# A hand-planned DeltaNet and MLP kernel on one core: the order of SP's and POOL's transfers, waits of transfers on TensorE, and the PSUM bank of two joins

## The chip, the cores and the metric

The kernel runs on one core of one Trainium2 chip. The metric is the device time in microseconds (us). The engines are named as the profile names them: PE (TensorE's products) with PEld (its weight loads), DVE (VectorE), ACT (ScalarE), POOL (GpSimd), and SP (SyncE, which here only issues transfers).

## The reference

```
k_n = k / (norm(k) + 1e-6)                          # per token
for t in range(S):
    y[t]  = q[t] @ state                            # y before the update
    old   = k_n[t] @ state
    state = state + beta[t] * outer(k_n[t], v[t] - old)
x  = y, heads side by side                          # (B, S, 384)
xn = (x - mean) / sqrt(var + 1e-6) * g_ln
out = x + relu(xn @ w_ch1) @ w_ch2                  # 384 -> 1536 -> 384
```

B = 4, H = 8, S = 768, D = 48, everything in float32. The first part is a recurrence over 768 tokens for each of the 32 pairs of batch and head; the second is a layer norm and a two-layer perceptron for each of the 3072 tokens.

## The kernel before, in words

**Chunks.** The recurrence is cut into 12 chunks of 64 tokens. Within a chunk it becomes matrix algebra: a Gram product of the keys (G, line 963, called by `gram`, line 978), products of queries and keys (also line 963), an inverse X of a unit triangular 64x64 matrix for each head, and then from the state: what the state gives for keys and queries (line 1160), the update u from X (lines 1196 and 1215), the output y (line 1222) and the state's increment (line 1232). The twelve states follow one another: a chunk's u needs the state that the chunk before has left. After y come the layer norm (lines 1266 to 1278), the transposes of its result (line 1310, on PE for chunks 0 to 2, by transfers for the later ones) and the perceptron `mlp(c)`: its first layer (line 1483 for c < 3, line 1416 with fewer products and more sums for the later), a relu on ACT (line 1492), and the second layer (line 1505 for c = 0, line 1584 for the later).

**The inverse, in three ways.** For chunk 0 it is made on PE by doubling: pairs of products E1, Z1 to E5, Z5 (lines 915 and 930), each in two halves, with masks on DVE (line 920), transposes on DVE (line 879) and copies on ACT (line 873) between them. For all other chunks it is made by rows on DVE, for 128 blocks at once (`rows_inverse`, line 1014): the Gram matrix is stored to memory (`gd<-gsb`), its diagonal blocks are gathered back by eight transfers so that each partition holds one block (`gb<-gd`), ACT takes the square root of the diagonal, the keys' norms (line 1026), DVE scales (lines 1027 to 1037) and works through the rows (line 1045 and 1050, in turn), and the result is stored (`xd<-xb`, line 1054) and gathered to its place (`xt<-xd`, line 1058). Chunk 1 has blocks of 16 rows, which `blocks_join` (line 1063, products at 1077 and 1082) makes into blocks of 32; chunks 2 and 3, 4 and 5, and so on are done in twos, in blocks of 32. `join` (line 1098) puts two blocks of 32 together: product e (line 1110), a copy on ACT, product z (line 1115), a copy on ACT. Its PSUM bank is `f2`, one of the perceptron's own, for chunks below `LATER` = 6, and half of `by`, where y is made, for the others; for these it is also emitted with the chunk's own step and not with `rows_inverse`.

**Weights.** They are held as words: ACT fetches pieces of 768 KB (`words<-in_moe_w_ch_dram`), and ACT (lines 730 and 738), DVE (735) and POOL (748) turn each into `w_sb`.

**What sets the order.** The program is not written in the order in which it runs. Class `Line` (line 75) is a planner: every group of instructions is added as a step with its engine, a cost, the keys that it reads and writes, a lag (so long it is held after its inputs are ready) and `t0`, the earliest time that the plan may start it. Due dates for the perceptrons (the list DUE; its last entry is URGENT, the margin from which an overdue small step goes ahead of a perceptron's products) are counted backwards to priorities. `run` then simulates the five engines, the rings of transfers, and the turns of 8 transfer semaphores, and picks steps one after another; in gaps on PE it puts filler products that compute nothing (`zeros`, line 1662). `emit` writes the steps sorted by planned start, and `in_this_order` (line 25) fixes that order on each engine. So a changed cost, lag, `t0` or due date acts on the chip only through the order of the instructions. `t0` of a transfer moves it in the plan and so in its queue; on the chip nothing holds it once its queue reaches it and its data and its semaphore are free.

SP issues nearly all transfers in one queue: raw keys (`load_raw`, four transfers for a chunk), q and v, blocks of q (`load_blocks`), `beta_b`, Gram stores, gathers, outputs. POOL issues the blocks of k for chunks 4 and up, between its own arithmetic, and ACT the words. All stand at line 555, the helper `dma`; a transfer is known in the trace by its names.

In before the raw keys of chunk 2 (to `kr`) and chunk 3 (to `tb`) have `t0` 27 and 29; of the eight gathers of chunk 1 six stand ahead of them in SP's queue and two behind.

Of the kernel before, what the change touches and what calls it, by code (L numbers as in the profile page):

```python
# [18 lines left out]
BK = 32  # L19
# [33 lines left out]
def dve(n):  # L53
    return 0.16 + 1.04e-3 * n
# [20 lines left out]
class Line:  # L75
# [313 lines left out]

        self.steps = every + self.fills  # L390

    def emit(self):
        for s in sorted(self.steps, key=lambda s: (s.start, s.n)):
            s.fn()


@with_exitstack
def kernel(
# [20 lines left out]
    nc = tc.nc  # L419
# [9 lines left out]
    TURNED = 4  # L429
    LNPE = 2  # L430
    GP = 2 * NP
    FROM, LATER = 3, 6
    TOK = 256
    WN = 768

# [76 lines left out]
    xld = dram.tile([128, KC, 4, 2 * BK], FP32, name="xld")  # L512
    xds = [dram.tile([128, BK, BK], FP32, name=f"xd{i}") for i in range(2)]

    line = Line()
    add = line.add
    TWO, BY = ([(n, b, g) for b in range(2) for g in range(2)] for n in ("two", "by"))
# [33 lines left out]

    def dma(eng, out_, in_, n, ns, r=(), w=(), **kw):

        cost = 0.65 if eng != "SP" else 0.45 if n <= 512 else 0.62
        add(eng, cost, lambda: QUEUE[eng].dma_start(out=out_, in_=in_), r, w, bulk=n * ns / 16e3, **kw)  # L555


# [382 lines left out]
    def turned(c, i, dst, dkey, **kw):  # L940
        add(
            "DVE", 1.24,
            lambda: nc.vector.transpose(  # L943
                dst.rearrange("p i (u t) -> p i u t", t=BK), tb[i].rearrange("p (h u d) -> p h u d", u=2, d=BK)
            ),
            tb_keys(i, "blk"), [dkey + (g,) for g in range(2)], **kw,
        )

    def key_half(c, hp, e):
# [64 lines left out]
    def rows_inverse(L, chunks, beta_l, xd, **kw):  # L1014
        gv, xv = (t.rearrange("p s t -> p (s t)")[:, 0 : L * L].rearrange("p (s t) -> p s t", t=L) for t in (gb, xb))
        gbk = [("gb", n) for n in range(8)]
        nb, ns = GH * L, 13.7 if L == BK else 11
        add("Pool", 0.1 + 0.85e-3 * L * L, lambda: nc.gpsimd.memset(xv, 0.0), [], ["xb"], after=MASK_SCRATCH, **kw)
        for n, (p0, c, rows, cols) in enumerate(spots(L, chunks)):
            dma(  # L1020
                "SP", gv[p0 : p0 + GH], gds[c % NG][rows, :, cols].rearrange("s h t -> h s t"),
                nb, ns, [("gd", c % NG)], [("gb", n)], **kw,
            )
        diag = lambda t: t.rearrange("p s t -> p (s t)")[:, 0 :: L + 1]
        nrm, db = nrm_b[:, 0:L], db_b[:, 0:L]
        add("ACT", 0.25, lambda: nc.scalar.sqrt(nrm, diag(gv)), gbk, ["nrm_b"], **kw)
        add("DVE", 0.15, lambda: nc.vector.tensor_scalar_add(nrm, nrm, 1e-6), [], ["nrm_b"], port=2, **kw)
        add("DVE", 0.35, lambda: nc.vector.reciprocal(nrm, nrm), [], ["nrm_b"], port=2, **kw)
        add("DVE", 0.2, lambda: nc.vector.tensor_tensor(out=db, in0=nrm, in1=nrm, op=ALU.mult), ["nrm_b"], ["db_b"], port=1, **kw)
        add(  # L1030
            "DVE", 0.2, lambda: nc.vector.tensor_tensor(out=db, in0=db, in1=beta_l[0], op=ALU.mult),
            beta_l[1], ["db_b"], port=1, **kw,
        )
        add("Pool", 0.25, lambda: nc.gpsimd.tensor_copy(out=diag(xv), in_=db), ["db_b"], ["xb"], **kw)  # L1034
        add(
            "DVE", dve(L * L),
            lambda: nc.vector.tensor_tensor(out=gv, in0=gv, in1=db[:, None, :].to_broadcast([128, L, L]), op=ALU.mult),
            ["db_b"], gbk, port=1, **kw,
        )
        for j in range(L - 1):  # L1040
            n, w = j + 1, L - 1 - j

            def row(j=j, n=n, w=w):
                t = tmp[:, 0 : n * w].rearrange("p (s t) -> p s t", t=w)
                nc.vector.tensor_tensor(  # L1045
                    out=t, in0=xv[:, 0:n, j : j + 1].to_broadcast([128, n, w]),
                    in1=gv[:, j : j + 1, j + 1 : L].to_broadcast([128, n, w]), op=ALU.mult,
                )
                rest = xv[:, 0:n, j + 1 : L]
                nc.vector.tensor_tensor(out=rest, in0=rest, in1=t, op=ALU.subtract)  # L1050

            add("DVE", 2 * dve(n * w), row, gbk, ["xb"], port=1, **kw)
        xdv = xds[xd].rearrange("p s t -> p (s t)")[:, 0 : L * L].rearrange("p (s t) -> p s t", t=L)
        dma("SP", xdv, xv, 128, 25 + L * L * 0.15, ["xb"], [("xd", xd)], **kw)
        for n, (p0, c, rows, cols) in enumerate(spots(L, chunks)):
            if L < BK:
                cols = slice(cols.start % BK, cols.start % BK + L)
            dma(
                "SP", xts[c % NX][rows, :, cols], xdv[p0 : p0 + GH].rearrange("h s t -> s h t"),
                nb, ns, [("xd", xd), ("xz", c % NX)], [("xq", c % NX, n % 8 if L < BK else n % 4)], **kw,  # L1060
            )

    def blocks_join(c, **kw):

        gs, xtc = gsbs[c % NG], xts[c % NX].rearrange("p h (b t) -> p h b t", b=2)
        gk = [("g", c % NG, g) for g in range(2)] + [("go", c % NG, e) for e in range(2)]
        xq = [("xq", c % NX, n) for n in range(8)]
        pe_, pz_ = (p.rearrange("p (h t) -> p h t", t=BK) for p in (f_[2], by[:, 0]))
        XN, ES = ([(n, 0), (n, 1)] for n in ("xn", "es"))
        XT = [("xt", c % NX, g) for g in range(2)]  # L1070
        add("DVE", dve(512), lambda: nc.vector.transpose(xnj, xtc[:, :, 0]), xq + XT, XN, **kw)

        def prod_e():
            for h in range(GH):
                for a in range(4):
                    b = BK * (a % 2)
                    nc.tensor.matmul(pe_[quad(a), h], gs[quad(a), h, b : b + BK], xnj[quad(a), h])

        def prod_z():
            for h in range(GH):  # L1080
                for a in range(4):
                    nc.tensor.matmul(pz_[quad(a), h], es[quad(a), h], xtc[quad(a), h, 0])

# [14 lines left out]
    def join(c, **kw):  # L1098
# [4 lines left out]
        add("DVE", dve(512), lambda: nc.vector.transpose(xnj, xt[:, :, 0:BK]), xq + [("xz", c % NX)] + [("xt", c % NX, g) for g in range(2)], [("xn", 0), ("xn", 1)], **kw)  # L1103
        p = bank.rearrange("p (h t) -> p h t", t=BK)
        c0 = 0 if c == 1 else BK

# [26 lines left out]
    def norms(c, **kw):  # L1133
        i = c % 2
        flat = gpads[c % NG].rearrange("p h t -> (p h t)")
        w = GH * C
        for e in range(2):
            own = flat[e * C * w : e * C * w + C * (w + 1)].rearrange("(s x) -> s x", x=w + 1)[:, 0:w:C]
            dma(
                "SP", ksum[i][half(e)], own, GH * C, 11, [("gd", c % NG)], [("ks", i, e)],  # L1140
                t0={1: 60.0, 2: 90.0, 3: 120.0}.get(c, 0.7), **kw,
            )
        kk = [("kn", i, n) for n in range(2)]
        add("ACT", 0.22, lambda: nc.scalar.sqrt(knrm[i], ksum[i]), [("ks", i, e) for e in range(2)], kk, **kw)
# [196 lines left out]
        return fbanks[turns[0] % 2] if not turns[1] else fbanks[turns[1] % 3]  # L1341


    DUE = [44.40, 70.70, 90.32, 129.22, 162.45, 201.63, 231.70, 268.25, 308.70, 351.43, 392.84, 417.04, 2.36, 1.27, 1.35, 26.71]
    line.URGENT = DUE[15]

    def due(c, t):
# [341 lines left out]
    def prep_g(m):  # L1689
        pr = 20 * m - 15  # L1690
        for c in (2 * m, 2 * m + 1):
            kt = (kts[c % NKT], ("kt", c % NKT))
            if c == 2:
                load_raw(c, pr=pr, t0=27.0)
                first_kt(kraws[2], raw_keys(2), *kt, PAIRS[3], pr=pr, t0=40.0)
            elif c == 3:
                keys = [("tb", 2, e, hp) for hp in range(2) for e in range(2)]
                load_raw(c, dst=tb[2], keys=keys, pr=pr, t0=29.0)
                first_kt(tb[2], keys + [("tbpad", 2)], *kt, PAIRS[3], pr=pr, t0=40.0)
            else:  # L1700
                load_blocks(2 * (c % 2), k, c, "Pool", pr=pr, t0={2: 80.0, 3: 120.0}.get(m, 40.0 * m - 20))
# [14 lines left out]
    for n, (p0, c, rows, cols) in enumerate(spots(BK, (0, 1))):  # L1716
# [1 line left out]
        dma(  # L1718
            "SP", beta_b[p0 : p0 + GH],
            beta[2 * e : 2 * e + 2].rearrange("g h (m s) -> (g h) m s", m=NSL)[:, :, t0 : t0 + BK],  # L1720
            96, 13.7, w=[("beta_b", n)], pr=5, t0=46.0,
        )

    def prep_x(m):
# [16 lines left out]
            join(c, pr=pr, lag=0.5)  # L1741
        recur(c, pr, lag=0.8)

    load_padded(1, q, 1, ("SP", "SP"), pr=8.2, t0=42.0)
    load_v(1, pr=8.1, t0=42.0)
    norms(1, pr=4)
    blocks_join(1, pr=3)
    join(1, pr=3)
# [22 lines left out]
    if PLAN is not None:  # L1771
        PLAN.append(line)
    with in_this_order(tc):
        line.emit()


# [28 lines left out]
```

## Time and profile before

| | |
|---|---|
| median of 5 runs | 560.1 us (558.41 to 561.62) |
| the profiled execution | 559.68 us |
| its span, first to last instruction | 558.0 us |
| mean granted clock of PE | 0.983 |
| PE busy | 527.5 us |
| last product ends | 553.56 us from the span's start |
| `gb<-gd`, 40 issues, 64 KB each in the median | 3.4 us from issue to landing |
| `words<-in_moe_w_ch_dram`, 10 issues, 768 KB | 5.9 us |

The profile is read by the span's own clock: a product "at 65.44" starts 65.44 us after the first instruction. In the chain of work that ended last, each line is a start, a duration and an engine with a line of the code; an engine's name with a q (SPq, ACTq) is the issue of a transfer by that engine, and DMA is the transfer itself. In a row of the timeline the bracket says how long the engine had stood idle and which instruction ended it. "issue" there means that nothing the profile records was waited for. PEclk is the clock that PE was granted, in tenths of full speed.

### The profile page before, as it was taken

The page shows a single profiled execution, that of the slowest core. Times are in us where ns is not written, and L with a number is a line of the kernel's source. Part 1 is how long each engine was busy: PE and PEld are TensorE (multiplying, and loading weights), DVE is VectorE, ACT ScalarE, POOL GpSimd, SP SyncE. Part 2 cuts the span into 40 slices and gives each one's busy share as a digit, 9 for nine tenths or more (in the row PEclk, how much of TensorE's full clock was granted, in tenths as well). Part 3 has the DMA queues.
Part 4 walks back from the last instruction along what each step waited for, and adds up shares of the span by engine and source line. Part 5 has one row for each costly group of instructions (what it writes and reads, how often), then busy time and mean ns, then how long its engine had stood idle before and what let it go on. Part 6 is the DMA issues. An engine that isn't in the chain of part 4 may idle for free.

```text
span 558.0 us, 23060 instructions
## 1 busy us (share of the span) xinstructions
PE 527.5 (95%) x10060; PEld 478.3 (86%) x10060; DVE 366.2 (66%) x884; ACT 191.3 (34%) x452; POOL 253.5 (45%) x399
## 2 busy tenths in 40 slices
PE   8777978999998999899999999999999999999996
PEld 5556756678987799899999999999999999999996
DVE  4686548972689946989858868668778436253331
ACT  4586634232242324232323423413313224323030
POOL 5251438306885656276260362453352612426242
PEclk9798989899999999999999999999999999999999
DMA  9866777188455767553742544734414410111101
GB/s 172 269 144 138 186 197 102 28 188 143 56 80 87 130 177 95 117 100 83 173 68 55 98 78 95 173 45 81 94 23 96 107 30 32 32 56 32 28 1 29
DMA packets 195973, 54.67 MB, mean 98 GB/s; under 512 B 186136, under 2 KB 189344, under 8 KB 195872
## 3 DMA queue, kind: packets, MB, share of 16 engines
q1 hardware_dynamic: 190112, 40.39, 37.6%
q10 hardware_dynamic: 3552, 9.63, 5.4%
q0 software_dynamic: 2208, 3.17, 3.8%
q8 instruction: 79, 1.29, 1.0%
q14 instruction: 22, 0.18, 0.1%
HBM read 36.38 MB, written 16.78 MB: 95 GB/s over the span
## 4 chain that ended last, share of the span: by engine, by line
PE 85%; DVE 5%; DMA 4%; issue 2%; ACT 2%; SPq 1%; POOL 0%; ACTq 0%; DVEq 0%; POOLq 0%
PE f L1584 28%; PE f L1416 25%; PE f L1483 6%; PE two L963 4%; PE f L1505 3%; PE by L1222 2%; PE two L1232 2%; PE by L1160 2%; PE two L1160 2%; PE two L1215 2%; DMA gd<-gsb 1%; DVE tmp L1045 1%; PE by L1110 1%; PE by L1115 1%; DVE xb L1050 1%
## 5 line engine op out<-in xcount | busy, mean ns | idle before, releaser
L1584 PE MATMUL f<-w_sb,h_all 128*128 128x192 f32 x396 | 95.1, 332 | 0.0
L1584 PE MATMUL f<-words,h_all 128*128 128x192 f32 x396 | 93.1, 328 | 0.0
L1570 POOL TENSOR_TENSOR h_all<-h_all 128x256 f32<-128x256 f32 x99 | 73.1, 744 | 40.7 <-PE f L1584 35.6
L1416 PE MATMUL f<-xnt,w_sb 128*128 128x128 f32 x648 | 88.0, 277 | 0.0
L1609 POOL TENSOR_TENSOR words<-h_all 128x128 f32<-128x128 f32 x66 | 30.8, 478 | 117.0 <-ACT h_all L1435 98.0
L1416 PEld LDWEIGHTS f<-xnt,w_sb 128*128 128x128 f32 x648 | 80.1, 192 | 0.7
L1438 DVE TENSOR_TENSOR h_all<-f,h_all 128x256 f32<-128x256 f32 x135 | 56.5, 421 | 33.5 <-PE f L1416 19.6
L1050 DVE TENSOR_TENSOR xb<-xb,tmp 128x60 f32<-128x60 f32 (+19 forms) x170 | 69.9, 411 | 5.8
L1045 DVE TENSOR_TENSOR tmp<-xb,gb 128x60 f32<-128x60 f32 (+19 forms) x170 | 65.9, 387 | 7.1 <-POOL xb L1034 4.5
L1584 PEld LDWEIGHTS f<-words,h_all 128*128 128x128 f32 x396 | 68.3, 190 | 0.4
L1584 PEld LDWEIGHTS f<-w_sb,h_all 128*128 128x128 f32 x396 | 66.4, 190 | 1.8 <-ACT words L1615 0.3
L1483 PE MATMUL f<-xnt,w_sb 128*128 128x256 f32 x216 | 52.5, 393 | 4.8 <-ACT h_all L1492 4.8
L1483 PEld LDWEIGHTS f<-xnt,w_sb 128*128 128x128 f32 x216 | 41.0, 195 | 12.9 <-ACT h_all L1492 4.4
L555 POOL DMA_DIRECT2D tb<-in_k_dram x64 | 41.6, 656 | 7.0 <-DVE kt L943 5.8
L1602 DVE TENSOR_TENSOR o<-f,x 128x192 f32<-128x192 f32 x33 | 11.7, 355 | 47.9 <-PE f L1584 22.8
L1435 ACT ACTIVATE h_all<-f 128x256 f32<-128x256 f32 x54 | 20.6, 381 | 53.4 <-PE f L1416 27.7
L1584 PE MATMUL f<-w_sb,words 128*128 128x192 f32 x132 | 32.5, 330 | 0.6 <-DVE o L1602 0.6
L1602 POOL TENSOR_TENSOR o<-o,words 128x192 f32<-128x192 f32 x22 | 13.3, 624 | 38.6 <-DVE words L1602 38.6
L748 POOL TENSOR_TENSOR w_sb<-words 128x768 uint32<-128x768 uint32 (+1 forms) x11 | 14.9, 1359 | 28.2 <-ACT words L738 18.4
L1492 ACT ACTIVATE h_all<-f 128x256 f32<-128x256 f32 x36 | 13.6, 382 | 38.7 <-PE f L1483 35.1
L1435 ACT ACTIVATE h_all<-h_all 128x256 f32<-128x256 f32 x54 | 22.2, 413 | 10.3 <-DVE h_all L1438 10.2
L825 POOL TENSOR_TENSOR v<-v,knrm 128x768 f32<-128x768 f32 x11 | 16.7, 1519 | 17.6 <-PE f L1416 10.0
(235 smaller groups left out, 940.5 us busy)
## 6 DMA issues: line engine op xcount, KB each, us to landing
words<-in_moe_w_ch_dram ACTq DMA_DIRECT2D x10, 768.0 KB, 5.9
gd<-gsb SPq DMA_DIRECT2D x11, 512.0 KB, 3.5
v<-in_v_dram SPq DMA_DIRECT2D x24, 192.0 KB, 4.5
out_dram<-o SPq DMA_DIRECT2D x48, 96.0 KB, 2.6
kr<-in_k_dram SPq DMA_DIRECT2D x46, 96.0 KB, 3.3
xld<-xlt SPq DMA_DIRECT2D x9, 384.0 KB, 3.6
xnt<-xld SPq DMA_DIRECT2D x36, 96.0 KB, 3.2
gb<-gd SPq DMA_DIRECT2D x40, 64.0 KB, 3.4
```

The source lines that it names most:

```text
L555: add(eng, cost, lambda: QUEUE[eng].dma_start(out=out_, in_=in_), r, w, bulk=n * ns / 16e3, **kw)
L963: nc.tensor.matmul(pair[hp][half(e ^ (hp & n)), (g * NP + j) * C : (g * NP + j + 1) * C], kt[drows(hp), l], rt[drows(hp), i],)
L1045: nc.vector.tensor_tensor(out=t, in0=xv[:, 0:n, j : j + 1].to_broadcast([128, n, w]), in1=gv[:, j : j + 1, j + 1 : L].to_broadcast([128, n ...
L1050: nc.vector.tensor_tensor(out=rest, in0=rest, in1=t, op=ALU.subtract)
L1416: nc.tensor.matmul(wide(p[:, 128 * n : 128 * n + 128]), w[:, f : f + 128], r, start=start and n == 0, stop=stop, skip_group_check=True)
L1435: add("ACT", act(256), lambda: nc.scalar.activation(to[0], p, ACTF.Relu), pk, to[1])
L1438: add("DVE", dve(256), lambda: nc.vector.tensor_tensor(out=to[0], in0=ps(p), in1=y[0], op=op), [*pk, *y[1]], to[1])
L1483: nc.tensor.matmul(p[:, 0:TOK], w1_sb[:, t, f * 128 : (f + 1) * 128], xnt[:, t], start=(t == 0), stop=(t == KC - 1))
L1570: add(eng, cost, lambda: e.tensor_tensor(out=out_, in0=x, in1=y, op=op), r, w, port=2 if eng == "Pool" else 1, pr=-2)
L1584: lambda f=f, t=start and f == 0: nc.tensor.matmul(p[:, 0:D2], lhs(f), rhs[:, f], start=t, stop=(f == F2 - 1), skip_group_check=True),
L1602: lambda: e.tensor_tensor(out=out_, in0=a, in1=b_, op=ALU.add), r, w, pr=pr,
L1609: lambda f=f + i: e.tensor_tensor(out=s3[f], in0=one(0, 0)[0](f), in1=one(1, 0)[0](f), op=ALU.subtract),
```

## The change

1. `emit` gets an additional dependency. If a step is a transfer of SP or POOL (not ACT) with a `t0` above 1.0, and the plan starts it less than 3.0 after its `t0`, it is made to wait on the chip for a PE step: the last among the eight latest PE steps whose planned end is not after the transfer's planned start. 37 transfers get such a wait, among them the raw keys of chunks 2 and 3, q and v of chunk 1, `beta_b`, q, v and the norms' sums of chunks 2 and 3, and the k blocks of chunks 4 to 7 on POOL.
2. `t0` of the raw keys of chunk 2 goes from 27 to 35, of chunk 3 from 29 to 37.5, of q and v of chunk 1 from 42 to 44, of `beta_b` from 46 to 48.
3. A list LAG gives lags to the square root (line 1026) of the first two `rows_inverse`, 2.00 each, and 0.72 to that of the later; the other entries are 0 or what was there before (0.5).
4. The planned cost of an SP issue becomes 0.45 below 384 packets and 0.65 from there (was 0.45 up to 512, else 0.62). Three due dates and URGENT are changed.
5. `LATER` goes from 6 to 4, so that the joins of chunks 4 and 5 use y's bank and come with the chunk's own step.

No product, copy or transfer is added or taken away but for fillers: 29 instructions of them before, 25 after. In the new order SP issues all eight gathers of chunk 1 ahead of the raw keys; then the keys, q and v of chunk 1, part of `beta_b`, the store of chunk 1's inverse (`xd<-xb`) ahead of the gathers of chunks 2 and 3, where it was behind them, and the gathers back (`xt<-xd`) mixed with the rest of those. On PE the transposes of chunk 2's keys and product G2, which stood between the halves of Z4 and of E5, come behind E5, the transposes ahead of Z5 and G2 behind it. On ACT the copies of Z5 come ahead of those of the Gram product and of keys, the square root of chunks 2 and 3 behind most of mlp(0)'s relus, and a fetch of words behind the layer norm's root. On DVE `xln` of chunk 2 comes ahead of a mask product (line 994) and of rows.

```diff
-    def emit(self):
+    def emit(self, tc):
+        block = tc.nc.cur_bb.bb.instructions
+        gate, ends = None, []
         for s in sorted(self.steps, key=lambda s: (s.start, s.n)):
             s.fn()
+            if s.eng == "PE":
+                ends.append((s.end, block[-1]))
+            if s.bulk is not None and s.t0 > 1.0 and s.eng != "ACT" and s.start < s.t0 + 3.0:
+                gate = [i for e, i in ends[-8:] if e <= s.start]
+                if gate:
+                    tc.add_manual_dep(
+                        block[-1], gate[-1].name,
+                        mybir.DependencyInfo(mybir.DependencyClass.Sync, mybir.DependencyReason.DATA), reason="paced",
+                    )
...
-    FROM, LATER = 3, 6
+    FROM, LATER = 3, 4
...
+    LAG = [2.00, 2.00, 0.72, 0.00, 0.50, 0.50, 0.00, 0.00]
...
-        cost = 0.65 if eng != "SP" else 0.45 if n <= 512 else 0.62
+        cost = 0.65 if eng != "SP" else 0.45 if n < 384 else 0.65
...
-        add("ACT", 0.25, lambda: nc.scalar.sqrt(nrm, diag(gv)), gbk, ["nrm_b"], **kw)
+        add("ACT", 0.25, lambda: nc.scalar.sqrt(nrm, diag(gv)), gbk, ["nrm_b"], lag=LAG[min(chunks[0] // 2, 2)], **kw)
...
-    DUE = [44.40, 70.70, 90.32, 129.22, 162.45, 201.63, 231.70, 268.25, 308.70, 351.43, 392.84, 417.04, 2.36, 1.27, 1.35, 26.71]
+    DUE = [44.40, 70.70, 90.32, 129.22, 162.45, 201.63, 230.26, 270.16, 308.70, 352.52, 392.84, 417.04, 2.36, 1.27, 1.35, 23.59]
...
-                load_raw(c, pr=pr, t0=27.0)
+                load_raw(c, pr=pr, t0=35.0)
...
-                load_raw(c, dst=tb[2], keys=keys, pr=pr, t0=29.0)
+                load_raw(c, dst=tb[2], keys=keys, pr=pr, t0=37.5)
...
-            96, 13.7, w=[("beta_b", n)], pr=5, t0=46.0,
+            96, 13.7, w=[("beta_b", n)], pr=5, t0=48.0,
...
-    load_padded(1, q, 1, ("SP", "SP"), pr=8.2, t0=42.0)
-    load_v(1, pr=8.1, t0=42.0)
+    load_padded(1, q, 1, ("SP", "SP"), pr=8.2, t0=44.0)
+    load_v(1, pr=8.1, t0=44.0)
```

The dates and lags in this code are those of the plan; none of them is a measured time.

More of the change, by code (lines that the diff above doesn't have):

```diff
@@ L945, in turned @@
             ),
-            tb_keys(i, "blk"), [dkey + (g,) for g in range(2)], **kw,
+            tb_keys(i, "blk"), [dkey + (g,) for g in range(2)], lag=LAG[6], **kw,
         )
@@ L1070, in blocks_join @@
         XT = [("xt", c % NX, g) for g in range(2)]
-        add("DVE", dve(512), lambda: nc.vector.transpose(xnj, xtc[:, :, 0]), xq + XT, XN, **kw)
+        add("DVE", dve(512), lambda: nc.vector.transpose(xnj, xtc[:, :, 0]), xq + XT, XN, lag=LAG[3], **kw)
         def prod_e():
@@ L1102, in join @@
         xq = [("xq", c % NX, n) for n in range(8)]
-        add("DVE", dve(512), lambda: nc.vector.transpose(xnj, xt[:, :, 0:BK]), xq + [("xz", c % NX)] + [("xt", c % NX, g) for g in range(2)], [("xn", 0), ("xn", 1)], **kw)
+        add("DVE", dve(512), lambda: nc.vector.transpose(xnj, xt[:, :, 0:BK]), xq + [("xz", c % NX)] + [("xt", c % NX, g) for g in range(2)], [("xn", 0), ("xn", 1)], **dict(kw, lag=LAG[4 + (c > 3)]))
         p = bank.rearrange("p (h t) -> p h t", t=BK)
@@ L1143, in norms @@
         kk = [("kn", i, n) for n in range(2)]
-        add("ACT", 0.22, lambda: nc.scalar.sqrt(knrm[i], ksum[i]), [("ks", i, e) for e in range(2)], kk, **kw)
+        add("ACT", 0.22, lambda: nc.scalar.sqrt(knrm[i], ksum[i]), [("ks", i, e) for e in range(2)], kk, lag=LAG[7], **kw)
         add("Pool", 0.2, lambda: nc.gpsimd.tensor_scalar_add(knrm[i], knrm[i], 1e-6), [], kk + [("kn", i)], **kw)
@@ L1773 @@
     with in_this_order(tc):
-        line.emit()
+        line.emit(tc)
 _INS = ['q', 'k', 'v', 'beta', 'moe_g_ln', 'moe_w_ch1', 'moe_w_ch2']
```

## The prediction

> **What bounds the kernel now.** I read the busy shares and the slices first, then the chain that ended last, then the gaps of TensorE and, in the stretch that the change touches, the waits and the chain in order of time. From the page:
>
> ```profile
> PE 527.5 (95%) x10060; PEld 478.3 (86%) x10060; DVE 366.2 (66%) x884; ACT 191.3 (34%) x452; POOL 253.5 (45%) x399
> ...
> PE   8777978999998999899999999999999999999996
> ...
> PEclk9798989899999999999999999999999999999999
> DMA  9866777188455767553742544734414410111101
> ...
> PE 85%; DVE 5%; DMA 4%; issue 2%; ACT 2%; SPq 1%; POOL 0%; ACTq 0%; DVEq 0%; POOLq 0%
> ```
>
> TensorE is the bound: 527.5 us busy of 558.0. A slice is 13.95 us. The holes and the reduced clock lie in the first eight slices, up to 112 us, while the DMA digits are high there; after slice 16 (223 us) the row is all nines. By the gaps between TensorE's instructions some 26 us are idle in all, and only 2.8 us of that after 226 us. No product is added or taken away by the change, so it can gain only what TensorE idles, what its filler products (line 1662) cover, and what half clock costs. That is spent in the first 226 us, and there I stay.
>
> Three stretches matter. The first is chunk 0's inverse, about 38 to 56 us. The timeline rows of TensorE:
>
> ```profile
> 44.65 0.69 PE L915 MATMUL two<-qt,gsb 64*64 64x64 f32 x32
> ...
> 48.69 0.39 PE L963 MATMUL f<-kt 48*64 48x64 f32 x11 [2.53 <-issue]
> ...
> 50.49 0.99 PE L930 MATMUL two<-xt,pt 64*64 64x64 f32 x32 [0.41 <-DVE pt L920]
> ```
>
> The first half of the E5 product (line 915) runs at 44.65, then comes Gram product G2 of the next chunk (line 963), in its middle 2.53 us with nothing waited for (code arriving), and only then E5's second half (48.86) and Z5 (49.40, 50.49 to 51.48). The second is mlp(0), where the chain in order of time reads:
>
> ```profile
> 68.21 1.30 POOL w_sb L748
> 69.51 2.17 DMA xd<-xb
> ...
> 72.05 5.49 DMA xt<-xd
> 77.54 0.02 issue
> 77.56 0.02 ACTq L555
> 77.58 0.04 issue
> 77.61 0.37 ACTq L555
> 77.99 0.05 issue
> 78.03 0.39 ACT h_all L1492
> 78.43 0.04 issue
> 78.47 4.30 PE f L1483 x12
> ```
>
> and the waits of ACT between 60 and 90 us, in sum, times and longest:
>
> ```profile
> ACT nrm_b L1026 <- DMA gb<-gd: 3.4, 1, 3.4
> ACT h_all L1492 <- DMA xt<-xd: 3.4, 1, 3.4
> ```
>
> ACT is queued behind transfers twice. Its square root for chunks 2 and 3 (line 1026, 71.57) stands ahead of a relu of mlp(0) and waits for gathers. Its weight fetch (line 555, 77.61) does not issue until `xt<-xd` has landed, although it shares no data with it: the issues use a limited set of transfer semaphores in turn, and the fetch's turn is held by that gather. TensorE then waits 1.18 us (71.85 to 73.03) and 2.61 us (75.86 to 78.47) for the relu, and the twelve products after the second gap take 4.30 us where the same twelve took 2.86 at 67.92. Nor is `xd<-xb` itself on time: its rows are ready at 60.15 and it is issued at 69.51, because SP spends 59.95 to 69.40 on eight gathers of the next two chunks. The third stretch is between a chunk's output and the next mlp: y1 ends at 109.08 and the first product of mlp(1) starts at 121.93; y2 ends at 161.06 and mlp(2) starts at 173.83.
>
> **The change part by part** (against the profiled 559.68).
>
> *Front: gathers of chunk 1 first, keys of chunks 2 and 3 later; −4.8, bounds −6 to −2.* In SP's queue all eight gathers now stand ahead of the raw keys (before: six at 23.48, the last two at 34.79, behind eight key issues of 0.65). TensorE's new order is Z4's halves without the key transposes between them (1.02 us gone from there), both halves of E5, the transposes, Z5, one filler, G2. From 44.65, less the 1.0 of the transposes, E5, copies and Z5 take what they took without G2's 0.99 + 2.53 ahead of the second half: Z5 ends near 47.2 to 48.2 and not at 51.48, 3.3 to 4.3 earlier. The code still has to arrive; I let half of the 2.53 come back: −3.0. ACT's copies of Z5 (line 873) ended 4.07 us after it (55.55), with a Gram copy and two key copies between them (1.53 waiting for the transposes of line 771); now they stand first: six copies of 0.38, 2.3 us, so −1.8. Ends: all of the code load comes back (−2); none, and all transposes hidden (−6).
>
> *SP's and ACT's queues in mlp(0); −5.2, bounds −5.2 to 0.* The store `xd<-xb` is moved ahead of the gathers of chunks 2 and 3 and the square root behind most of the relus. That removes 1.18 + 2.61 + (4.30 − 2.86 = 1.44). What is late next is the fetch itself, moved behind the LN's root. No gain at all if another transfer holds its turn.
>
> *What is then late: ahead of mlp(1); +4.7, bounds 0 to +4.7.* The 12.85 us between y1 and mlp(1) are filled now. If mlp(0) ran ahead, less of its second layer is left: in the new order seven products of line 1505 stand there (0.71 each: the trace shows two records for each, eight records in 2.85 us), 5.0 us, two Grams at 1.10 and two transposes at 0.49, 8.2 us in all, and seven fillers where there were none. With the way through VectorE, ACT and the transposes as long as it is now, 12.85 − 8.2 = 4.7 come back. Its shortest seen length is y0's: 58.71 to 65.44, 6.73, with which nothing would come back; but VectorE has chunk 1's to 3's rows (lines 1045, 1050) between, so I take the upper end.
>
> *Ahead of mlp(2); −1.4, bounds −3.9 to 0.* The line that carries it:
>
> ```profile
> 171.55 1.05 PE L1310 MATMUL by<-ident,xln 128*128 128x128 f32 x6 [1.40 <-DVE xln L1278]
> ```
>
> VectorE runs a mask product (line 994, 1.22) and two row steps (168.15 to 171.01) ahead of `xln`; in the new order `xln` comes first. The stall goes; up to 3.9 if the fillers shrink too.
>
> *Waits added; +1.1, bounds 0 to +2.6.* 37 transfers of SP and POOL now wait for a TensorE instruction. Behind the waiting issue stands the rest of that queue: at SP q and v of chunk 1, `beta_b`, the Gram store and the gathers; at POOL the last weight conversions (line 748, 1.47 each) behind chunk 4's k blocks, which wait for mlp(0)'s second layer. For the keys of chunk 2 the gates are E4's halves (38.54, 39.05), for those of chunk 3 E4 and Z4; such a transfer lands 3.4 to 4.5 after its issue, so chunk 2's last one by 43 to 45, about when its transposes now come. The trace has no such wait. Nothing, if the keys land in 3.4; the 1.1 between the two landings, if in 4.5; and a conversion more, 2.6, if POOL's queue decides too. I take 1.1, since the transposes come close to the landing and the conversions are wanted only by mlp(1).
>
> *Half clock after a new gap; +1.0, bounds 0 to +1.7.* Gaps of 2.71, 2.53, 2.61 us are each followed by 3.4 us at 0.5 (PEclk over 50 to 54 us 0.59, over 78 to 82 us 0.57), at 1.44 to 1.69 us each. Where the holes ahead of mlp(1) are filled this costs nothing; I take two thirds of one. The Trainium skill (TensorE: Matmul & The Clock Gate, Part 1) names a longer idle window, about 3.4 us, before the clock halves; here gaps of 2.5 to 2.7 were enough. By the page's rule this term would be 0.
>
> *Joins of chunks 4 and 5 in y's bank; 0, bounds −1 to +1.5.* Same products (211.53 to 221.92, both chunks' ahead of y4 at 222.38); now chunk 5's come behind y4. TensorE waited for nothing between them, since products of mlp(2) stand there; in the new order products of the same mlp do. The nearest gaps are 1.51 of code at 223.74, taken as the loss, and two small ones at 255.93 and 336.06 (0.68, 0.64), in sum 1.3, of which a gain of 1 is the most.
>
> Sum: −4.8 − 5.2 + 4.7 − 1.4 + 1.1 + 1.0 + 0 = −4.6, so 555.1 in the profiled execution, and 555.5 as a median, which lies 0.42 above it before (560.1 against 559.68).
>
> The Trainium skill (DMA: Bandwidth & Descriptors, Issuing engines are not separate DMA queues) says that transfers from any engine interleave on the same 16 engines and that more issuing engines save only issue time. Taken alone it speaks against this change, since the bytes stay the same; the store that is ready at 60.15 and issued at 69.51 shows that the order within one queue counts here.
>
> **Rivals.**
>
> *Slower: the held transfers hold ACT.* A gated transfer keeps its turn until its TensorE product is done and its bytes have landed. If ACT reaches its second fetch (now ahead of copies that TensorE needs) while that turn is held, ACT stands still, as at 77.61. Longest landing seen: 9.86 us (`tb<-in_q_dram`, issued at 36.64). Price up to 9.9: −4.6 + 9.9 = +5.3, 565.4. It decides from the point where the transfer lands over 4.6 us after ACT is there. For it: the wait at 77.61, and `beta_b`, whose six issues took 6.98 us from 43.25, 1.16 each against 0.65 of a key, so turns were short there already. Against it: with the keys held back fewer transfers of the front share the engines, and the same bytes may land sooner.
>
> *All given back: about 560.1.* The chain through chunk 1 to 3 may be the true bound, and every microsecond won early turns into fillers; −4.8 − 5.2 come back ahead of mlp(1) and mlp(2). For it: the new fillers. Against it: stalls of 1.18 and 2.61 have nothing to do with that chain.
>
> *More is kept: 550.8.* Nothing comes back ahead of mlp(1), if its way takes nearer 6.73 than 12.85: 555.5 − 4.7.
>
> *The waits do nothing.* Where a transfer is issued later than its product anyway (those held to 105 and 120 in the plan go out from 112 on), the gate is empty; then the order alone acts, and the time is within the first case.
>
> **How the numbers follow.** Likeliest case 0.50 (551 to 558.5; 0.46 faster, 0.04 the same). More kept 0.12, faster. Given back 0.15 (0.02, 0.10, 0.03). ACT held 0.23 (0.03 the same, 0.20 slower). Together faster 0.60, same 0.17, slower 0.23; 0.3%, 1.7 us, is about what a measurement of this kernel can tell from no change. Range 551 to 563: it leaves out the upper part of the held case (0.14) and the lowest of the kept one (0.06). The likeliest case's own range is 551 to 558.5.
>
> **What would show it.** Z5 ends near 48; no wait of line 1026 ahead of a relu and no wait of a fetch on `xt<-xd`; the first product of line 1483 near 60.7; fillers and a gap ahead of mlp(1), which starts about 8 to 13 us after y1; by 300 us the same products come 4 to 5 us earlier than before, and from there on the two traces run in parallel. It is wrong if ACT waits for a transfer anew, if TensorE waits for a key transpose, or if mlp(1) starts where it did.

## The result, and the profile after

| | before | after |
|---|---|---|
| median of all runs | 558.54 us (91 runs, 552.91 to 564.80) | 559.01 us (51 runs, 554.21 to 563.48) |
| ratio to before, 95% interval | | 1.0014 (1.0002 to 1.0027) |
| profiled execution, span | 559.68, 558.0 us | 559.42, 557.6 us |

A drop of 4.6 us was forecast; the change costs 0.8 us (0.14% of 558.5). Runs of one kernel differ by several us, so a ratio rests on many of them, and a difference of two spans is read to about 2 us.

The page of the changed kernel, for the rows shown of before:

```profile
PE 525.7 (94%) x10052; PEld 475.9 (85%) x10052; DVE 367.8 (66%) x884; ACT 191.6 (34%) x452; POOL 257.2 (46%) x399
...
PE   7667998999999999998999999999999999999996
...
PEclk9998998999999999989999999999999999999999
DMA  9846866389365577246671645352524131122101
...
PE 76%; DVE 8%; DMA 7%; issue 3%; POOL 3%; ACT 2%; SPq 0%; ACTq 0%; DVEq 0%; POOLq 0%
```

PE's sixth slice (70 to 84 us) goes from 7 to 9: the waits in mlp(0) are gone. The first three are emptier by one each. In the chain PE has fallen from 85% to 76%; VectorE, transfers and POOL took the place.

Lines of code are 14 higher in the changed kernel (1483 is now 1497), and a few more in some experiments. The timeline of TensorE in the front, changed kernel:

```profile
39.73 0.69 PE L929 MATMUL by<-qt,gsb 64*64 64x64 f32 x32 [0.57 <-ACT xt L887]
43.41 1.06 PE L785 MATMUL f<-ident,kr 128*128 128x128 f32 x8 [2.99 <-DMA kr<-in_k_dram]
44.40 0.89 PE L944 MATMUL f<-xt,pt 64*64 64x64 f32 x32
...
52.97 0.68 PE L1236 MATMUL two<-u,pt 64*64 64x48 f32 x32 [1.47 <-DVE u L1215]
```

E5's second half now runs at 39.73 and not at 48.86, without G2 ahead of it. Then TensorE stands for 2.99 us, because the transposes ahead of Z5 want chunk 2's keys, which a wait had held back. TensorE had been ready for them at 40.42. The waits of ACT between 60 and 90 us, same kernel:

```profile
ACT h_all L1506 <- PE f L1497: 5.6, 6, 2.8
ACT h_all L744 <- DMA beta_b<-in_beta_dram: 1.8, 1, 1.8
ACT nrm_b L1040 <- issue: 1.4, 1, 1.4
```

The two waits of 3.4 are gone. A new one is there: ACT stands 1.8 us until `beta_b` has landed, whose turn its fetch of words needs, and `s_all`, queued behind, comes late; TensorE idles 0.96 us for it at 63.02. That is the rival with the held turns, at a tenth of its price here (0.96 of 9.9; 1.85 in e4 below).

To see where time goes, count for every product the median distance to the next one on its line in before, nothing for fillers, and call what TensorE's time exceeds this by lost. The windows are fixed stretches of the span, so 1 us may belong to a neighbour. The last column is the experiment e4 below.

| us of the span | before | after | e4, keys not held |
|---|---|---|---|
| 0 to 60 | 37.0 | 36.3 | 34.2 |
| 60 to 80 | 9.6 | 2.2 | 3.8 |
| 80 to 110 | 11.1 | 12.1 | 11.3 |
| 110 to 122 | 2.5 | 6.1 | 6.4 |
| 122 to 175 | 14.5 | 15.3 | 14.1 |
| 175 to 270 | 22.6 | 23.9 | 23.0 |
| 270 to the end | 38.7 | 39.7 | 39.4 |
| sum | 136.0 | 135.6 | 132.1 |

By this count 8.1 us are won by 80 us in the changed kernel and given back in several places, the largest 3.6 us ahead of mlp(1). The starts say the same: mlp(0) at 60.27 (65.44 before), y1's end 107.81 (109.08), mlp(1) 120.28 (121.93), mlp(2) 169.43 (173.83). Each column is one execution, and the front of one kernel moves by more than its total: in e16 below, whose order is that of before up to 86 us, TensorE waited 4.42 us for chunk 1's norms (0.51 in before) and mlp(0) started at 69.67, not at 65.44.

### The profile page after: what moved, and what is told of

Read it like the earlier page. It is cut to its first block, busy times and chain, and to the rows that moved or that the text cites. A ratio compares the mean times of both kernels' runs of the same rounds, so it can differ in the third digit from the quotient of the medians.

```text
span 557.6 us, 23081 instructions
## 1 busy us (share of the span) xinstructions
PE 525.7 (94%) x10052; PEld 475.9 (85%) x10052; DVE 367.8 (66%) x884; ACT 191.6 (34%) x452; POOL 257.2 (46%) x399
## 4 chain that ended last, share of the span: by engine, by line
PE 76%; DVE 8%; DMA 7%; issue 3%; POOL 3%; ACT 2%; SPq 0%; ACTq 0%; DVEq 0%; POOLq 0%
PE f L1598 28%; PE f L1430 25%; PE f L1497 4%; PE two L977 3%; DVE xb L1064 2%; DVE tmp L1059 2%; PE by L1236 2%; PE two L1229 2%; PE by L1174 2%; PE two L1174 2%; PE by L1129 2%; PE by L1124 2%; PE two L1246 2%; DMA xt<-xd 2%; DMA words<-in_moe_w_ch_dram 1%
## 5 line engine op out<-in xcount | busy, mean ns | idle before, releaser
L1598 PE MATMUL f<-w_sb,h_all 128*128 128x192 f32 x396 | 97.4, 336 | 0.0
L1430 PEld LDWEIGHTS f<-xnt,w_sb 128*128 128x128 f32 x648 | 79.5, 192 | 3.4 <-issue 1.7
L1064 DVE TENSOR_TENSOR xb<-xb,tmp 128x60 f32<-128x60 f32 (+19 forms) x170 | 73.5, 432 | 5.8
L1497 PE MATMUL f<-xnt,w_sb 128*128 128x256 f32 x216 | 49.8, 383 | 0.0
L1497 PEld LDWEIGHTS f<-xnt,w_sb 128*128 128x128 f32 x216 | 40.2, 190 | 6.0
L1446 ACT COPY h_all<-f 128x256 f32<-128x256 f32 x27 | 10.0, 372 | 44.2 <-PE f L1430 43.7
L839 POOL TENSOR_TENSOR v<-v,knrm 128x768 f32<-128x768 f32 x11 | 16.3, 1483 | 16.4 <-DMA v<-in_v_dram 9.5
```

The source lines that it names most:

```text
L1430: nc.tensor.matmul(wide(p[:, 128 * n : 128 * n + 128]), w[:, f : f + 128], r, start=start and n == 0, stop=stop, skip_group_check=True)
L1497: nc.tensor.matmul(p[:, 0:TOK], w1_sb[:, t, f * 128 : (f + 1) * 128], xnt[:, t], start=(t == 0), stop=(t == KC - 1))
L1598: lambda f=f, t=start and f == 0: nc.tensor.matmul(p[:, 0:D2], lhs(f), rhs[:, f], start=t, stop=(f == F2 - 1), skip_group_check=True),
```

## The experiments

Each was run 6 to 12 times beside before on the same chip; the ratio is to before, with its 95% interval. The changed kernel's own is 1.0014 (1.0002 to 1.0027).

| run | ratio | interval |
|---|---|---|
| e1 no waits | 0.9953 | 0.9925 to 0.9981 |
| e2 waits alone, on before | 1.0041 | 1.0007 to 1.0075 |
| e4 keys of chunk 2 not held | 0.9951 | 0.9916 to 0.9987 |
| e4b the same again | 0.9934 | 0.9903 to 0.9964 |
| e5 gathers back first | 1.0048 | 1.0015 to 1.0081 |
| e6 gathers in first | 1.0012 | 0.9981 to 1.0043 |
| e7 e4 and e5 | 0.9962 | 0.9931 to 0.9993 |
| e3 LATER = 6 in the changed kernel | 1.0230 | 1.0196 to 1.0264 |
| e8 LATER = 4 alone, on before | 1.0122 | 1.0088 to 1.0156 |
| e9 e4, layer norm first, no fillers | 1.0004 | 0.9970 to 1.0037 |
| e10 e4, no fillers | 0.9970 | 0.9935 to 1.0005 |
| e11 e4, layer norm first | 1.0002 | 0.9972 to 1.0032 |
| e12 e4, store of chunk 1 late | 0.9955 | 0.9922 to 0.9988 |
| e13 e4, rows cut, no fillers | 0.9872 | 0.9824 to 0.9921 |
| e14 e4, rows cut | 0.9898 | 0.9862 to 0.9934 |
| e16 rows cut, on before | 1.0025 | 0.9996 to 1.0054 |

**e1, no waits.** The condition for a wait is never true; the order of all engines is that of the changed kernel.

```diff
-            if s.bulk is not None and s.t0 > 1.0 and ...
+            if False and s.bulk is not None and s.t0 > 1.0 and ...
```

> The changed kernel with its order unchanged and the 37 added waits left out. Three theories of where the gain went. A: the inverse of chunk 1 comes back too late (xt<-xd lands 9 us after its first issue), so chunk 1's chain sets mlp(1). B: VectorE, full from 85 us on with rows of chunks 2 and 3, sets it. C: it is lost after 235 us, with the joins of chunks 4 and 5. Here all three expect that the 2.99 us for which TensorE waits for kr go, and that mlp(0) begins up to 3 us earlier than 60.27. A and B expect no more than 1 us of it in the total, since transfers or rows decide later; C expects the 3 us in the total (about 556). If the held transfers made room for others, the gathers land later and it is slower by 1 to 3.

0.9953. The order without the waits is faster than before, the order with them is not; the difference in the total, 0.0061 or 3.4 us, is the size of the 2.99 us that are gone. But its profiled execution does not show it in the front. Where TensorE waited for the keys, two gaps have come in which nothing recorded was waited for:

```profile
45.16 0.21 PE L944 MATMUL f<-xt,pt 64*64 64x64 f32 x1 [2.15 <-issue]
...
49.17 0.26 PE L1210 MATMUL by<-v,xt 64*64 64x48 f32 x2 [1.09 <-issue]
```

mlp(0) starts at 61.99, later than 60.27 and against what all three theories expected.

**e2, the waits alone.** `emit` of the changed kernel put into before.

> The kernel before with only the added waits (its own order, t0 and joins). If the waits by themselves help by keeping transfers apart, words and gathers land sooner and it is 1 to 3 us faster than before. If they only hold SP's queue, it is the same or up to 3 us slower: q, v and beta_b of chunk 1 go out later and push the gathers of chunks 2 and 3, which stood ahead of xd<-xb. Theory A expects slower by the time that xd<-xb goes out after 69.51.

1.0041: the waits help nothing of themselves; 0.4 to 4.2 us slower by the interval. VectorE's transpose for chunk 1's blocks waits 9.0 us for `xt<-xd`, where it waited 5.0.

**e4, one set of four waits.** Only the four transfers of chunk 2's raw keys lose theirs; 33 waits stay.

```diff
-            if s.bulk is not None and s.t0 > 1.0 and ...
+            if s.bulk is not None and s.name != "keys2" and s.t0 > 1.0 and ...
...
-                load_raw(c, pr=pr, t0=35.0)
+                load_raw(c, pr=pr, t0=35.0, name="keys2")
```

> The changed kernel, only the four raw-key transfers of chunk 2 without a wait. They go out behind the last gather at 28 and not from 34.93. TensorE's wait of 2.99 us for kr should go, Z5 end near 43.5 and mlp(0) begin near 57.5. A: rows and xd<-xb earlier by up to 1, total within 1 us of the changed kernel. B: the same. C: 3 us less in the total.

0.9951, and again:

> The kernel with the keys of chunk 2 not held once more, as the reference on the same chip for the next three: about 0.995 of before.

0.9934. Four waits out of 37 carry all that e1 showed. In e4 TensorE goes from E5 to the transposes without a wait:

```profile
41.08 0.69 PE L929 MATMUL by<-qt,gsb 64*64 64x64 f32 x32 [0.57 <-ACT xt L887]
41.71 1.09 PE L785 MATMUL f<-ident,kr 128*128 128x128 f32 x8
```

The same holds over more executions. In the four that hold these keys in the changed front (the changed kernel, e5, e6 and e3 below) TensorE waits 2.99, 3.95, 3.18 and 4.38 us ahead of these transposes and mlp(0) starts at 60.27 to 63.26; in the nine that free them and keep the other waits TensorE waits for no key there and mlp(0) starts at 57.34 to 60.12. SP's queue, first the changed kernel, then e4:

```profile
22.09 5.91 SPq L569 DMA_DIRECT2D gb<-gd  x8
34.93 2.67 SPq L569 DMA_DIRECT2D kr<-in_k_dram  x4
```

```profile
23.20 6.19 SPq L569 DMA_DIRECT2D gb<-gd  x8
29.44 2.63 SPq L569 DMA_DIRECT2D kr<-in_k_dram  x4
```

The queue is empty at 28 in the first and stands until 34.93. And then the keys meet ACT's fetch of 768 KB, issued at 35.94. The median landings, issued between 34 and 44 us in the changed kernel:

```profile
words<-in_moe_w_ch_dram ACTq DMA_DIRECT2D x1, 768.0 KB, 6.1
kr<-in_k_dram SPq DMA_DIRECT2D x4, 96.0 KB, 6.4
```

and between 28 and 44 us in e4:

```profile
words<-in_moe_w_ch_dram ACTq DMA_DIRECT2D x1, 768.0 KB, 4.6
kr<-in_k_dram SPq DMA_DIRECT2D x4, 96.0 KB, 3.8
```

Held to a quiet moment in the plan, the keys went out in a busy one: 6.4 us to landing and not 3.8. The fetch alone does not make that. In e4 the keys of chunk 3 go out beside it (38.20, the fetch at 37.22) and take 4.5; in e1 both sets of keys go out one behind the other, 28.24 to 34.08, ahead of the fetch (36.82), and take 4.2 and 3.8. In the changed kernel both sets and the fetch meet, and all land late: 6.4, 6.8 (chunk 3) and 6.1. The Trainium skill (DMA: Bandwidth & Descriptors, Issuing engines are not separate DMA queues) says that transfers of different issuers interleave on the same engines. That fits; no run here moves the fetch alone.

**e5 and e6, the order of two sets of gathers.** Theory A held that chunk 1's inverse comes back late: its store is issued at 57.44 and not at 69.51, yet VectorE's transpose of the blocks starts at 81.83 (78.73 before). e5 puts all `xt<-xd` ahead of all `gb<-gd` of chunks 2 and 3 in SP's queue, e6 the other way round.

```diff
+        last = max(s.start for s in self.steps if s.name == "back1")
+        for s in self.steps:
+            if s.name == "in2":
+                s.start = max(s.start, last + 1e-3)
         for s in sorted(self.steps, key=lambda s: (s.start, s.n)):
```

> The changed kernel, with all eight gathers back (xt<-xd) in SP's queue ahead of the eight gathers of chunks 2 and 3 (gb<-gd), which stood ahead of and among them. A: xt lands by 70 to 73, the products of line 1091 start near 75 and not at 82.59, y1 ends 5 to 7 us earlier, and the total falls by 3 to 5. B: the square root of chunks 2 and 3 comes after 81.2, rows end later, xln of chunk 1 does not come earlier than 116.9 and the total is the same or up to 3 slower. C: the same.

> The changed kernel with the gathers of chunks 2 and 3 (gb<-gd) all ahead of the gathers back (xt<-xd); the store xd<-xb stays ahead of both. A: xt lands later than now, the products of line 1091 start at 83 to 86, total 1 to 3 slower. B: the square root of chunks 2 and 3 comes up to 8 us earlier than 81.2, VectorE's rows end earlier, xln of chunk 1 near 113, total 1 to 3 faster. C: the same.

In e5 the transpose starts at 73.61, 8 us earlier, and y1 ends at 109.44, 1.6 later than in the changed kernel; the total is not faster (1.0048). Theory A falls as stated, with 3 to 5 us to win. That the way back decides nothing is not shown, because e5 brings a new stall: ACT's square root now waits 3.89 us for the gathers of chunks 2 and 3, a relu stands behind it, and TensorE idles:

```profile
84.91 2.87 PE L1523 MATMUL f<-w_sb,h_all 128*128 128x384 f32 x4 [2.92 <-ACT h_all L1510]
```

In e6 the square root came at 84.08, not earlier as B had it, and the total stayed (1.0012); it told nothing of B. There ACT, with a fetch of words next, stood 5.85 us until a gather had landed, and TensorE 2.50 us for the relu behind it.

**e7, both.**

> The changed kernel with both edits: keys of chunk 2 not held, and gathers back ahead of the gathers in. A: the 3 us of the keys and the 3 to 5 of the gathers add up in part, 4 to 7 us faster than the changed kernel, about 553. B: as with the gathers alone, the same or slower. C: 3 us.

0.9962, no better than e4 alone; the stall of e5 is there again (2.37 us). Against e5, which differs from it only in the four waits, it is 0.0086 or 4.8 us faster by the ratios: freeing these keys pays in a second order too.

**e3 and e8, the joins of chunks 4 and 5.** One constant each, but the plan is made anew with it.

> The changed kernel with LATER = 6 again: joins of chunks 4 and 5 in the bank of the perceptron and with their rows; the order up to chunk 2 is the same. A and B: within 1 us of the changed kernel, since what is lost by 135 us stays lost. C: the 0.88 us of code and the half clock after it (242 to 246) go, about 1.9 us, with some of the gap of 1.72 at 259, so 2 to 3 us faster than the changed kernel.

> The kernel before with LATER = 4 alone. C: slower by 2 to 4, from gaps and half clock behind y4 as in the changed kernel. A and B: within 1 us of before.

Both slower, by 2.3% and 1.2%. Theory C, that the old place would win 2 to 3 us, falls as stated. But in e8 the order has changed from the start (a gap of 5.86 us at 75.81, long before chunk 4), and in e3 from chunk 2 on, with gaps of 2.07 us for POOL's `h_all` at 205.02 and 2.69 us for VectorE's `o` at 262.69. They measure a new plan, not the joins; what the joins alone cost stays open.

**e9 to e11, between y1 and mlp(1).** Theory D, formed here: the order is fixed, so the layer norm's place behind rows and the seven fillers are paid on the chip. All three start from e4.

```diff
+        y = max(s.start for s in self.steps if s.name == "y1")
+        last = max(s.start for s in self.steps if s.name == "xln1")
+        for s in self.steps:
+            if s.name == "row2" and y < s.start < last:
+                s.start = last + 1e-3
         for s in sorted(self.steps, key=lambda s: (s.start, s.n)):
+            if s.name == "fill" and 100.0 < s.start < 114.0:
+                continue
```

> The changed kernel with the keys of chunk 2 not held (as in the kernel with free keys, 0.995 of before), and between y1 and mlp(1) the layer norm of chunk 1 ahead of the rows of chunks 2 and 3 on VectorE, and the seven fillers left out there. Theory D, formed after the first runs: the instruction order is fixed, so what the plan puts between y1 and mlp(1) is paid on the chip: VectorE's rows ahead of xln, and seven fillers. D expects xln 4 us earlier and mlp(1) 3 to 4.5 us earlier after y1 (12.5 now), 2 to 4 us in the total, about 0.989 of before. Against D: rows finished 4 us later set the joins of chunks 2 and 3, and nothing is left in the total.

> As before it, but only the seven fillers left out and VectorE's order unchanged. D expects that the fillers alone cover a wait: TensorE then idles for xln, the total is the same within 1 us of the kernel with free keys, or up to 1.7 slower if the clock halves after the gaps. If the fillers themselves hold mlp(1), it is 2 to 4 faster.

> As before it, but only VectorE's order changed (layer norm of chunk 1 ahead of the rows), the seven fillers kept. D expects that mlp(1) cannot come much earlier, since the fillers are executed whether they are needed or not: 0 to 1.5 us faster than the kernel with free keys. If xln alone sets mlp(1), 3 to 4 us faster.

In e9 mlp(1) starts 10.0 us after y1's end and not 12.2, at 114.86. But see what TensorE meets next, e9:

```profile
114.86 1.56 PE L1504 MATMUL f<-xnt,w_sb 128*128 128x256 f32 x6 [0.46 <-ACT xnt L1347]
120.05 1.48 PE L984 MATMUL two<-qt,kt 48*64 48x64 f32 x64 [3.63 <-DVE qt L964]
```

VectorE, having done the layer norm first, is late with the rows, and behind them with the transpose of q (line 964); TensorE waits 3.63 us for that, mlp(1)'s last first-layer product ends 2 us later than in e4 (139.40, 137.41), and nothing is won: 1.0004, and with the fillers kept (e11) 1.0002, which had been expected at 0 to 1.5 us faster. Both are about 2 us slower than e12 below, which ran on the same chip and is as fast as e4. Without fillers alone (e10) the total is that of e4 within the intervals: they cover a wait and cost none of their own. D falls in the form that one place is to blame; the wait moves along VectorE's queue.

**e12, the store of chunk 1 behind the gathers in.**

> The changed kernel with the keys of chunk 2 not held, and the store of chunk 1's inverse (xd<-xb) behind the eight gathers of chunks 2 and 3, as it stood in the kernel before; the gathers back follow it. The prediction gave 4.05 us to this place (2.61 + 1.44). If that is so, it is 2 to 4 us slower than the kernel with free keys, with the products of line 1091 waiting until 84 to 87. If the products of mlp(0) fill that time, it is within 1 us.

0.9955, as e4. (In this kernel the store takes memory that POOL has already cleared for the next pair, so what comes back is not chunk 1's inverse.) The place to which 4.05 us had been put is worth nothing in this order: products of mlp(0) fill the time. What the total owes to ACT's queue is thus not the store's place; the square root behind the relus was not tried alone.

**e13, e14, e16: less work on VectorE.** What remained was theory B in a wider form: VectorE as a whole is full from 82 to 122 us.

```diff
             def row(j=j, n=n, w=w):
+                if chunks[0] == 2 and j > 15:
+                    return
```

> The kernel with free keys and without the seven fillers, and the last 15 of the 31 row steps of chunks 2 and 3 left out (their inverses are then not complete): the rows from 85 us on cost VectorE about 10 us less, the order of all else is the same. Theory B, in the form that the runs left: VectorE is full from 82 to 122 us, and its rows, not one instruction's place, set mlp(1) and what follows. B expects mlp(1) 8 to 10 us after y1 (12.2 now) and 2 to 4.5 us less in the total. If VectorE is not what bounds this stretch, within 1 us.

> The same with the seven fillers kept. B expects less of it, since 4.6 us of fillers stand between y1 and mlp(1) and are executed in any case: 0 to 2 us faster than the kernel with free keys.

> The kernel before with the same 15 row steps of chunks 2 and 3 left out. There the second layer of mlp(0) fills the 12.85 us between y1 and mlp(1), without a filler. If VectorE's rows bound only where the front has run ahead, the total is within 1.5 us of before; if they bound before too, 2 to 4 us faster.

0.9872 and 0.9898 against 0.9934 of e4b on the same chip: 3.5 and 2.0 us less, as B said. The intervals of the ratios overlap; the means of the runs themselves lie 3.6 ± 2.2 and 1.8 ± 1.4 us below e4b's (two standard errors). mlp(1) starts 10.0 and 11.2 us after y1's end, where e4b has 12.0. On before the same cut wins nothing (1.0025). So VectorE's rows bound this stretch where the front has run ahead, and only there. Windows of the changed kernel (busy of PE, PEld, DVE, ACT, POOL; clock; DMA share; GB/s):

```profile
70.00:80.00 10.00, 10.00 (x104) 8.04 (x103) 1.16 (x3) 4.32 (x8) 2.93 (x2) 1.00 0.81 185
80.00:90.00 10.00, 6.67 (x269) 4.75 (x268) 7.38 (x15) 5.68 (x10) 6.73 (x8) 0.96 0.41 97
90.00:100.00 10.00, 10.00 (x210) 6.92 (x210) 9.48 (x22) 2.71 (x5) 9.53 (x14) 0.87 0.84 123
100.00:110.00 10.00, 9.94 (x273) 6.57 (x271) 9.62 (x17) 1.77 (x4) 4.28 (x5) 1.00 0.27 34
110.00:120.00 10.00, 8.93 (x155) 6.43 (x156) 9.69 (x30) 3.89 (x9) 0.00 (x0) 1.00 0.84 182
```

and of e13:

```profile
100.00:110.00 10.00, 10.00 (x255) 6.81 (x248) 6.17 (x14) 3.17 (x7) 4.23 (x5) 1.00 0.29 47
110.00:120.00 10.00, 8.10 (x215) 6.34 (x214) 6.23 (x10) 3.18 (x9) 0.45 (x1) 1.00 0.85 210
```

In the changed kernel VectorE works 1.16 of the ten us from 70 on, and over 9.4 of each ten from 90 on. Its rows of chunks 2 and 3 begin at 86.60, where they began at 83.12 before: TensorE runs ahead, VectorE's rows do not. They wait for the square root, which ends at 81.49 (71.83 before), and for POOL; no run brought their start forward (87.64 in e5, 90.06 in e6).

## Why the prediction was wrong

**The waits were mis-sized; this is the step that failed.** "Waits added; +1.1, bounds 0 to +2.6" stands on keys that land 3.4 to 4.5 us after their issue. That row came from keys issued at 27.71 to 34.74 in before. Held, they went out together with chunk 3's keys and ACT's fetch and took 6.4, and TensorE waited 2.99. The last of them was issued at 37.0: with 3.4 to 4.5 it would have landed at 40.4 to 41.5, and TensorE, ready at 40.42, would have waited 0 to 1.1, the very term. (That it landed at 43.4, inside the forecast "43 to 45", is luck: its gate, E4's first half, ran at 34.15 and not at 38.54.) In the total the four waits are worth 0.0063 to 0.0080 of the time (1.0014 less 0.9951 and 0.9934), 3.5 to 4.5 us; the middle is above the bound of 2.6, though by the intervals it is 1.4 to 6.3. The other 33 cost nothing that can be measured (e1 against e4, to about 2 us). The rival that was to end slower had the right start, a held transfer, and the wrong victim: ACT's fetch behind a held turn cost 0.96 us (1.85 in e4, 2.50 in e6), not 9.9. The right place had been named, "if TensorE waits for a key transpose", but not priced as a rival.

**The front** (−4.8) was right in direction: mlp(0) starts 5.17 us earlier in spite of the stall, 7.48 in e4, 5.87 in e4b and 3.45 in e1. With a spread of this size its own worth cannot be told closer. That code still has to arrive was right too: e1 has 2.15 us of it in the place of the wait.

**SP's and ACT's queues** (−5.2): the waits went, and what is lost from 60 to 80 us fell by 7.4, which holds fillers too. But e12 shows that the store's place was not needed for it. That a square root ahead of a relu costs what it waits for showed again in e5 (2.92) and e7 (2.37).

**Ahead of mlp(1)** (+4.7): the reason given, a way as long as before through VectorE, was right: 12.47 us from y1's end to mlp(1), 12.85 before; the table shows 3.6 given back there and 1.0 from 80 to 110. That it would not be shorter was argued then from the rows; e13 and e14 against e4b bear it out. e9 and e11 show that it is not won by bringing the layer norm forward.

**Ahead of mlp(2)** (−1.4): the stall of 1.40 for `xln` is gone, and mlp(2) starts 9.69 us after y2's end (12.77 before), but from 122 to 175 us 0.8 more is lost than before; by this count nothing came of it.

**Half clock** (+1.0): the term did not come. The mean granted clock over the runs is 0.983 after and 0.980 before (51 runs, and the 119 of before beside the experiments), so the clock cost some 1.7 us less (0.003 of 558) and not 1.0 more. One reading under it was off as well: behind the gap of 2.71 in before the clock is at 0.51 from 20 to 27 us, near 6.8 us at half and not 3.4. **The joins** (0, up to +1.5): from 175 to 270 us 1.3 more is lost. In that stretch stand two gaps in which nothing recorded was waited for, 0.88 us at 241.65, within a join's product, and 1.72 at 259.08; e1 has the first and not the second. Whether the joins' place causes them was not settled. Another 1.0 us after 270 has no cause that was tested.

By the sum, −5.7 without the waits was forecast, and e4 gives −2.7 and −3.7 (0.9951 and 0.9934 of about 558.5). VectorE is not what is missing there: its term ahead of mlp(1) was put at 4.7 and came at 4.1 in e4 (80 to 122 us in the table). The 2 to 3 us that are missing lie in several places of the table, none over 1.5 us, and no run assigns them. With the held keys on top, all is gone. The rival "all given back" described the total, by another way than the true one.

A faster version is in hand: the changed order with the keys of chunk 2 not held, 0.9951 and 0.9934 of before, beats both kernels.

## What to carry to other kernels

A transfer's landing time belongs to the moment in which it goes out: price a held transfer with what else will be in flight then, what is held beside it included, not with the row that it has now, and look at whom it serves first. When TensorE is made to run ahead, find the engine whose work does not move with it (here VectorE's rows, idle at 70, full from 82 on); bringing one of its steps forward only hands the wait to the next. In a planned kernel a constant cannot be taken back to test one edit, since the whole order follows it; move or cut single steps in the finished order.

## What was not expected of the hardware

A short gap can cost clock. The gap of 0.88 us at 241.65 in the changed kernel is followed by these windows (columns as above, the clock third from the end):

```profile
240.00:245.00 5.00, 4.12 (x81) 3.74 (x74) 3.88 (x8) 1.15 (x2) 0.73 (x1) 0.77 0.57 130
245.00:250.00 5.00, 5.00 (x142) 4.27 (x141) 2.02 (x5) 0.00 (x0) 1.46 (x2) 0.89 0.35 78
```

(1 − 0.77) × 5 + (1 − 0.89) × 5 = 1.7 us of clock missing, 3.4 us at half. The gap of 1.72 at 259.08 was followed by full clock. The same gap of 0.88 stands in e6 (at 245.30, the clock from 245 to 250 is 0.69) and in e1 and e4 (at 240.06 and 239.12, full clock from 235 to 245). So its length does not decide. The Trainium skill (TensorE: Matmul & The Clock Gate, Part 1) gives an idle window of about 3.4 us for the drop and says that the window runs free of the program; the length of the stretch agrees, and the gap was a quarter of it. In the trace's record of the clock the half-clock stretches of the changed kernel begin at 44.75, 54.99, 89.12 and 242.72, which is 3, 10 and 45 steps of 3.413 us apart; in before (19.98, 50.70, 78.01, 98.49) it is 9, 8 and 6. So within an execution they keep a beat. What decides which gap costs, no run here tests.

Most gaps of TensorE in which nothing recorded was waited for end shortly after code has landed. The trace has 16 KB packets on an instruction queue (q8, 78 or 79 in each execution). Of 94 such gaps over 0.6 us between 14 and 300 us, in all 18 traces, 83 end 1.2 to 1.9 us after the end of such a packet; for the 2.53 us of before the packet ends at 47.26 and TensorE goes on at 48.69. The other 11, the 1.72 at 259.08 among them, all lie between 251 and 263 us and end 3.4 to 4.3 us after one; what they wait for is open.
